# Attention and MLP on one Trainium2 core: unit 1's transposes in other PSUM banks, and an MLP step that splits its weights before its activation

## The chip, the core and the metric

The kernel runs on one core of a Trainium2 chip. Its engines are TensorE (PE, with its weight loads PEld), VectorE (DVE), ScalarE (ACT), GpSimd (POOL) and SyncE (SP); SP, ACT and POOL also issue transfers, named SPq, ACTq and POOLq. The metric is device microseconds of one execution. The profile is of one execution, and its span is the time from its first to its last instruction.

## What is computed

```
# decayed linear attention over blocks of 64, 2 x 8 heads, 768 tokens, 64 wide
intra = (qb @ kb.T * Dmask) @ vb ;  inter = (qb * lam_pow) @ kv_state
kv_state = lam**block * kv_state + (kb * rev_pow).T @ vb
x = attn_out as (1536 tokens, 512)
# MLP, 512 -> 2048 -> 512
h = max(x @ w_in, 0) ;  x = (h * h) @ w_out
# 8 experts, one per token by argmax(x @ w_gate), 512 -> 1024 -> 512
out[mask] = gate * sigmoid(x @ w_output_gate)[e] * (max(x[mask] @ w1[e], 0) @ w2[e])
```

All inputs arrive in fp32, apart from the MLP's two weights, which arrive as 64-bit floats and are converted on the chip.

## The kernel before

The program is written out in the order in which each engine takes its instructions (`manual_schedule`): an engine runs its own list strictly in that order and waits where an operand or a buffer isn't ready. Where a tile of a pool is given out again, its first writer waits for the last reader of the old one.

**Attention** runs over 12 units u (6 chunks of 128 tokens by 2 batches). Each has these steps: T(u) (`emit_T`) transposes q and k on PE into the PSUM tile psT, of which there is one, and ACT copies it to SBUF (four copies of 64x256 for q at L269, one of 128x512 for k at L272) and then issues the load of v (`load_v`, L190). S(u) (`emit_S`, L293) multiplies k by q into two PSUM tiles, of which there is one set, and DVE multiplies them by the decay mask into sm (L295). O(u) (`emit_O`) adds state by q (L312, from unit 2 on) and sm by v (L317); ACT writes the result's rounded part to xTh (L320), DVE the rest to xTl (L321). St(u) (`emit_St`, L343) updates the state. The loop over u runs T(u+2), S(u+1), O(u), St(u). Ahead of the loop stand T(0), T(1) and S(0), with warm-up products of the identity between them (`warm_pe`, L208) whose result is not used. q and k are loaded by SP (`load_qk`), four units ahead.

**The MLP** runs in three chunks of 512 tokens, each with 16 steps f over the hidden width, s = 16 chunk + f. Products are made with operands split in a rounded high and a low part: w_in's block into wih (a cast on ACT, L359) and wil (a subtraction, L360), by `split_in`; w_out's into woh and wol, by `split_out`. mm1(s) has 12 products of 128x512 (L372), mm2(s) 12 (L492). Between them `act1(s)` makes relu (r) and square (g) and splits g into gh (ACT) and gl (DVE). r and g have one buffer each, gh, gl, woh and wol two. mm2(s-2) stands behind mm1(s) on PE. In chunk 0 the weights are still arriving: SP loads pieces into four staging tiles st, ACT scales a piece (L134), DVE shifts and combines it (L135, L138, L142, the last two through `flush`), and only the end of L142 frees the staging tile for another load. wol is made by DVE in chunk 0 and by POOL after it.

After the MLP come the last chunk's routing (an early gather on POOL, L729 and L730, whose rows PE transposes at L741) and the experts.

Of the kernel before, what the change touches and what calls it, by code (L numbers as in the profile page):

```python
# [9 lines left out]
F32 = mybir.dt.float32  # L10
# [14 lines left out]
def attn_moe_kernel(ctx, tc, q, k, v, lam, w_in, w_out, w_gate, w_ogate, w1, w2, out):  # L25
    nc = tc.nc
    B, H, S, D = q.shape
# [159 lines left out]
    def load_v(u):  # L187
        b, c = units[u]
        tv = ldv.tile([P, H, D], F32, tag="v", name="v")
        nc.scalar.dma_start(out=tv, in_=v[b, :, c * P:(c + 1) * P, :].rearrange("h s d -> s h d"))  # L190
        qkv[u].append(tv)
# [14 lines left out]
    def warm_pe(n):  # L206
        for i in range(n):
            nc.tensor.matmul(out=pw_[:, i % HP, :], lhsT=ident, rhs=ident, start=True, stop=True)  # L208
# [43 lines left out]
    def emit_T(u):  # L252
        qt, kt = qkv[u][0:2]
        b, c = units[u]
        psT = pT.tile([P, 2, 2, HP, D], F32, tag="psT", name="psT")
        for hp in range(HP):
            for a in range(2):
                sl = slice(a * D, (a + 1) * D)
                nc.tensor.transpose(psT[:, a, 0, hp, :], qt[sl, hp, :], ident[sl, sl])
        for hp in range(HP):  # L260
            for a in range(2):
                sl = slice(a * D, (a + 1) * D)
                nc.tensor.transpose(psT[:, a, 1, hp, :], kt[sl, 2 * hp:2 * hp + 2, :].rearrange("p h d -> p (h d)"),
                                    ident[sl, sl])
        qT, kT = qT2[u % 2], kT2[u % 2]
        kv = kT.rearrange("p h (g t) -> p g h t", g=2)
        for a in range(2):
            for r in range(2):
                nc.scalar.copy(out=qT[a * D:(a + 1) * D, :, r::2], in_=psT[r * D:(r + 1) * D, a, 0])  # L269
                if u == a == r == 0:  # L270
                    load_v(u)
        nc.scalar.copy(out=kv, in_=psT[:, :, 1])  # L272
        if u > 0:
            load_v(u)
        kTs[u] = kT
        if c > 0:
            qd = wa.tile([P, HP, P], F32, tag="qd", name="qd")
            nc.gpsimd.tensor_tensor(out=qd, in0=qT, in1=lrow, op=ALU.mult)
            qds[u] = qd
        if c < NCH - 1:  # L280
            kd = wa.tile([P, H, D], F32, tag="kd", name="kd")
            nc.gpsimd.tensor_tensor(out=kd, in0=kt, in1=mask[:, :, P - 1:P].to_broadcast([P, H, D]), op=ALU.mult)
            kds[u] = kd
# [109 lines left out]
    def split_in(s, eng=nc.vector):  # L393
        f = s % NF
        wis[s] = split(wiF[:, :, f * P:(f + 1) * P], "wi", [P, KC, P], eng)
# [30 lines left out]
    powers(2, 32)  # L426
    emit_T(0)
    powers(32, P + 1)
    for t in state:
        nc.vector.memset(t, 0.0)  # L430
    warm_pe(4)
    load_qk(3)
    emit_T(1)
    emit_S(0)
    decays(0)
    decays(1)
    for u in range(NU):

        emit_tmp(u)
        wload(WL[u])  # L440
        if u + 4 < NU:
            load_qk(u + 4)
        if u + 2 < NU:
            emit_T(u + 2)
        if u == NU - 3:
            nc.sync.dma_start(out=tab.rearrange("(p n) w -> p (n w)", p=P), in_=tabi)
            sqk.close()
            sp[0] = sab.enter_context(tc.tile_pool(name="sp", bufs=2, side="right", reuse_waits="tile"))
        if u == NU - 2:
            split_in(0)  # L450
        if u < NU - 1:
            emit_S(u + 1)
        flush()
        if u == NU - 2:
            split_in(1)
        if u == NU - 1:
            mm1(0)
        emit_O(u)
        emit_St(u)
        if u == NU - 1:  # L460
            split_in(2)
        rest_ += wconv(WA[u], pO if u < NU - 3 else None)
# [352 lines left out]
    for s in range(NS + LAG):  # L815
        if s < NS:
            if s >= 2:
                mm1(s)
            early = 1 <= s < NF
            act1(s, lambda: (split_out(s - 1) if s else None, split_in(s + 2) if early else None, flush()))  # L820
        elif s == NS:
            split_out(s - 1)
        if NF <= s < NS - 2:
            split_in(s + 2)
        if wc[0] < NPC:
            wload(2)
            rest_ += wconv(2)
            if wc[0] == NPC:
                for i in range(4):
                    load_w1(i)  # L830
                    load_w2(i)
        if s >= LAG:
            mm2(s - LAG)
            ch, f = divmod(s - LAG, NF)
            if f == NF - 1:
                evac(ch)
            if ch > 0:
                for job in side.get(f, ()):
                    job(ch - 1)
            if ch == NCK - 1 and f == 10:  # L840
                slot_idx(slice(0, NSL), slice(0, 1))
        if s - 2 * NF in range(1, 9):
            i, j = divmod(s - 2 * NF - 1, 2)
            (split1, split2)[j](i)
        if s == NS - 1:
            early_gather()
            route_base(NCK - 1)
# [278 lines left out]
```

## Time and profile before

| | us |
|---|---|
| median of 3 runs | 556.07 (554.93 to 558.4) |
| the profiled execution | 556.97 |
| its span | 555.3 |
| PE busy | 539.7 (97%) |
| DVE busy | 336.2 (61%) |
| ACT busy | 303.6 (55%) |
| POOL busy | 148.3 (27%) |

Busy time is summed over the whole span, so it doesn't say which wait ends last in one stage; that is read from the chain of waits (followed back from the last instruction) and from the timeline of the stage. In the timeline a row's bracket is the time for which its engine stood idle before it, and what ended that.

### The profile page before, as it was taken

To read this page: it belongs to the slowest core of one execution; us is meant where nothing else is said; L and a number is where in the kernel's file an instruction comes from. 1 tells how busy PE (TensorE), PEld (TensorE's weight loads), DVE (VectorE), ACT (ScalarE), POOL (GpSimd) and SP (SyncE) were. 2 spreads that over 40 slices of the span, in tenths; PEclk is the share of its full clock that TensorE was granted. 3 is DMA by queue.
4 is the path that set the end of the run, shared out by engine and by line. 5 is a ranking of instruction groups with operands and counts; after the bars stand their busy time and mean duration, and the time that the engine had idled before them with its cause. 6 is when DMAs were issued, how large, how long until landed. Compare 5 with 4: busy or idle time off the path is not lost.

```text
span 555.3 us, 9744 instructions
## 1 busy us (share of the span) xinstructions
PE 539.7 (97%) x3599; PEld 460.7 (83%) x3599; DVE 336.2 (61%) x714; ACT 303.6 (55%) x577; POOL 148.3 (27%) x166
## 2 busy tenths in 40 slices
PE   7999999999999999999999989999999999999994
PEld 7899777778888878888888878889888889888983
DVE  3568998989645643344583327948264948975610
ACT  4668667776543444454554424447274857884610
POOL 8697000000021142312133250440313142240101
PEclk9999999999999999999999999999999999999998
DMA  8998545556500000000000003999538568930000
GB/s 201 218 244 224 152 154 200 180 192 231 221 1 2 24 34 19 1 0 1 19 20 19 21 17 129 377 199 394 183 127 284 206 201 262 293 123 20 10 21 25
DMA packets 75044, 72.88 MB, mean 131 GB/s; under 512 B 30181, under 2 KB 61029, under 8 KB 74976
## 3 DMA queue, kind: packets, MB, share of 16 engines
q1 hardware_dynamic: 58288, 59.91, 33.7%
q0 software_dynamic: 4064, 8.91, 5.0%
q10 hardware_dynamic: 12624, 3.15, 2.5%
q8 instruction: 43, 0.70, 0.5%
q14 instruction: 25, 0.20, 0.1%
HBM read 65.84 MB, written 9.29 MB: 135 GB/s over the span
## 4 chain that ended last, share of the span: by engine, by line
PE 73%; issue 12%; DVE 4%; DMA 4%; POOL 2%; ACT 2%; SPq 1%; POOLq 0%; ACTq 0%; DVEq 0%
PE acc L492 22%; PE ps L372 22%; PE ph L927 10%; PE ea L949 9%; DMA out_dram<-y,sidx 2%; PE ps L293 2%; PE po L312 1%; PE po L317 1%; DMA v<-in_v_dram 1%; DMA k<-in_k_dram 1%; POOL out_dram L959 1%; PE px L705 1%; SPq L182 1%; PE pt L906 1%; PE pt L343 1%
## 5 line engine op out<-in xcount | busy, mean ns | idle before, releaser
L360 POOL TENSOR_TENSOR wol<-woF,woh 128x512 fp32r<-128x512 f32 x32 | 41.1, 1285 | 222.8 <-ACT woh L359 222.8
L492 PE MATMUL acc<-gh,wol 128*128 128x512 f32 x192 | 76.4, 398 | 1.7 <-POOL wol L360 1.7
L927 PE MATMUL ph<-xh,xTh 128*128 128x192 f32 (+2 forms) x256 | 76.9, 301 | 0.9 <-DVE xl L912 0.4
L372 PE MATMUL ps<-xTh,wih 128*128 128x512 f32 x192 | 76.5, 398 | 0.0
L492 PE MATMUL acc<-gh,woh 128*128 128x512 f32 x192 | 75.0, 391 | 0.8 <-ACT woh L359 0.8
L372 PE MATMUL ps<-xTh,wil 128*128 128x512 f32 x192 | 74.9, 390 | 0.1
L492 PE MATMUL acc<-gl,woh 128*128 128x512 f32 x192 | 74.8, 390 | 0.0
L372 PE MATMUL ps<-xTl,wih 128*128 128x512 f32 x192 | 74.8, 389 | 0.0
L927 PE MATMUL ph<-xh,xTl 128*128 128x192 f32 (+2 forms) x256 | 74.7, 292 | 0.0
L927 PE MATMUL ph<-xl,xTh 128*128 128x192 f32 (+2 forms) x256 | 74.3, 292 | 0.0
L942 DVE SCALAR_TENSOR_TENSOR hl<-ph,hh 128x384 fp32r<-128x384 f32 (+1 forms) x64 | 34.5, 539 | 61.8 <-ACT hh L941 61.7
L390 DVE TENSOR_TENSOR gl<-g,gh 128x512 fp32r<-128x512 f32 x48 | 33.2, 691 | 58.8 <-ACT gh L389 58.8
L389 ACT CAST gh<-g 128x512 fp32r<-128x512 f32 x48 | 29.8, 620 | 52.7 <-PE acc L492 45.2
L927 PEld LDWEIGHTS ph<-xh,xTh 128*128 128x128 f32 x256 | 48.6, 190 | 7.0 <-DVE hl L942 4.9
L379 ACT ACTIVATE r<-ps 128x512 f32<-128x512 f32 x48 | 28.6, 595 | 44.7 <-PE ps L372 44.4
L941 ACT ACTIVATE hh<-ph 128x384 fp32r<-128x384 f32 (+1 forms) x64 | 30.9, 483 | 37.2 <-PE ph L927 34.0
L927 PEld LDWEIGHTS ph<-xl,xTh 128*128 128x128 f32 x256 | 48.6, 190 | 0.8
L927 PEld LDWEIGHTS ph<-xh,xTl 128*128 128x128 f32 x256 | 48.8, 191 | 0.2 <-DVE xTl L806 0.2
L886 POOL DMA_INDIRECT xg<-x1d,gidx x21 | 23.6, 1123 | 87.1 <-PE pt L906 62.3
L492 PEld LDWEIGHTS acc<-gh,wol 128*128 128x128 f32 x192 | 36.0, 188 | 12.9 <-DVE wol L360 3.7
L959 POOL DMA_INDIRECT out_dram<-y,sidx x23 | 23.6, 1028 | 76.9 <-ACT y L958 74.4
L806 DVE TENSOR_TENSOR xTl<-w1r,xTh 128x512 fp32r<-128x512 f32 x64 | 43.8, 689 | 0.1
(191 smaller groups left out, 1153.2 us busy)
## 6 DMA issues: line engine op xcount, KB each, us to landing
w1r<-in_moe_w_dram SPq DMA_DIRECT2D x32, 512.0 KB, 6.3
w2r<-in_moe_w_dram SPq DMA_DIRECT2D x32, 512.0 KB, 6.6
st<-in_moe_w_in_dram SPq DMA_DIRECT2D x16, 512.0 KB, 4.3
st<-in_moe_w_out_dram SPq DMA_DIRECT2D x16, 512.0 KB, 3.6
q<-in_q_dram SPq DMA_DIRECT2D x24, 128.0 KB, 4.5
k<-in_k_dram SPq DMA_DIRECT2D x12, 256.0 KB, 4.6
v<-in_v_dram ACTq DMA_DIRECT2D x12, 256.0 KB, 4.3
x1d<-xr SPq DMA_DIRECT2D x12, 256.0 KB, 2.0
```

The source lines that it names most:

```text
L360: eng.tensor_tensor(out=lo, in0=src, in1=hi.bitcast(F32), op=ALU.subtract)
L372: nc.tensor.matmul(out=ps, lhsT=w_[:, kk, :], rhs=x_[:, kk, tk], start=n == 0, stop=n == 3 * KC - 1)
L379: nc.scalar.activation(out=r, in_=ps, func=AF.Relu)
L389: nc.scalar.copy(out=gh, in_=g)
L390: nc.vector.tensor_tensor(out=gl, in0=g, in1=gh.bitcast(F32), op=ALU.subtract)
L492: nc.tensor.matmul(out=acc[ch][cb], lhsT=w_[:, cs], rhs=x_, start=f == 0 and i == 0, stop=f == NF - 1 and i == 2)
L806: eng.tensor_tensor(out=lo, in0=src, in1=hi.bitcast(F32), op=ALU.subtract)
L927: nc.tensor.matmul(out=ps[:, 0:N], lhsT=w_[:, kk, :], rhs=x_[:, kk, 0:N], start=n == 0, stop=n == 3 * KC - 1)
L941: nc.scalar.activation(out=hh[:, f, ts_], in_=ps[:, ts_], func=AF.Relu)
L942: nc.vector.scalar_tensor_tensor(out=hl[:, f, ts_], in0=ps[:, ts_], scalar=0.0, in1=hh[:, f, ts_].bitcast(F32), op0=ALU.max, op1=ALU.subtract)
L949: nc.tensor.matmul(out=ea[j], lhsT=h_[:, f, js], rhs=w_, start=f == 0 and i == 0, stop=f == NF2 - 1 and i == 2)
L959: nc.gpsimd.indirect_dma_start(out=outs[j][:, :], out_offset=bass.IndirectOffsetOnAxis(ap=sidx[:, j, e:e + 1], axis=0), in_=ys[j], in_offs ...
```

## The change

```
     def emit_T(u):
-        psT = pT.tile([P, 2, 2, HP, D], F32, tag="psT", name="psT")
+        if u == 1:
+            psa = [pm.tile([P, 2, HP, D], F32, tag="ps", name="psT1") for _ in range(2)]
+        else:
+            psT = pT.tile([P, 2, 2, HP, D], F32, tag="psT", name="psT")
+            psa = [psT[:, a] for a in range(2)]
...
+        if u == 0:
+            warm_pe(2)
...
+        copy = nc.vector.tensor_copy if u == 1 else nc.scalar.copy
         for a in range(2):
             for r in range(2):
-                nc.scalar.copy(out=qT[a * D:(a + 1) * D, :, r::2], in_=psT[r * D:(r + 1) * D, a, 0])
-                if u == a == r == 0:
-                    load_v(u)
-        nc.scalar.copy(out=kv, in_=psT[:, :, 1])
-        if u > 0:
-            load_v(u)
+                copy(out=qT[a * D:(a + 1) * D, :, r::2], in_=psa[a][r * D:(r + 1) * D, 0])
+        if u == 1:
+            for a in range(2):
+                copy(out=kv[:, a], in_=psa[a][:, 1])
+        else:
+            copy(out=kv, in_=psT[:, :, 1])
+        load_v(u)
...
-    for t in state:
-        nc.vector.memset(t, 0.0)
-    warm_pe(4)
+    warm_pe(7)
     load_qk(3)
     emit_T(1)
     emit_S(0)
+    for t in state:
+        nc.vector.memset(t, 0.0)
...
-        if u == NU - 2:
-            split_in(0)
         if u < NU - 1:
             emit_S(u + 1)
         flush()
-        if u == NU - 2:
-            split_in(1)
+        if NU - 3 <= u < NU - 1:
+            split_in(u - (NU - 3))
...
             if s >= 2:
                 mm1(s)
-            early = 1 <= s < NF
-            act1(s, lambda: (split_out(s - 1) if s else None, split_in(s + 2) if early else None, flush()))
-        elif s == NS:
-            split_out(s - 1)
+            if 1 < s <= NF:
+                split_out(s - 1)
+            if 1 <= s < NF:
+                split_in(s + 2)
+            act1(s, flush if s < NF else lambda: split_out(s))
+            if s == 0:
+                split_out(0)
```

T(1) gets two tiles of the pool that O and mm1 use, its copies go to DVE, the state's zeroing goes behind the first sm, and there are five more warm-ups. The splits of w_in's first two blocks come one unit earlier. In chunk 0 both splits of a step stand ahead of relu and square; in chunks 1 and 2 a step splits its own w_out block and not that of the step before.

On DVE, at the program's start (ca_142 is the mask in the first row and qT elsewhere, ca_141 is kT, ca_143 and ca_144 are the states), before:

```order
L215 SCALAR_TENSOR_TENSOR ca_142<-ca_141,ident 128x128 x8
L430 MEMSET ca_143 128x512
L430 MEMSET ca_144 128x512
L295 TENSOR_TENSOR sm<-ps,ca_142 128x4x128 x4
L321 TENSOR_TENSOR xTl<-po,xTh 128x4x128
```

and now:

```order
L215 SCALAR_TENSOR_TENSOR ca_142<-ca_141,ident 128x128 x8
L276 COPY ca_142<-psT_233 64x256 x2
L276 COPY ca_142<-psT_234 64x256 x2
L279 COPY ca_141<-psT_233 128x4x64
L279 COPY ca_141<-psT_234 128x4x64
L303 TENSOR_TENSOR sm<-ps,ca_142 128x4x128 x2
L442 MEMSET ca_143 128x512
L442 MEMSET ca_144 128x512
```

Six copies stand ahead of sm(0), and the two memsets between sm(0) and sm(1). On ACT, at the same place, before:

```order
L196 DMA ca_141<-in_lam_dram 128x8
L269 COPY ca_141<-psT 64x256
L190 DMA v<-in_v_dram 128x8x64
L269 COPY ca_141<-psT 64x256 x3
L272 COPY ca_141<-psT 128x2x4x64
L269 COPY ca_142<-psT 64x256 x4
L272 COPY ca_141<-psT 128x2x4x64
L190 DMA v<-in_v_dram 128x8x64
```

and now:

```order
L196 DMA ca_141<-in_lam_dram 128x8
L276 COPY ca_141<-psT 64x256 x4
L281 COPY ca_141<-psT 128x2x4x64
L190 DMA v<-in_v_dram 128x8x64 x2
L276 COPY ca_141<-psT 64x256 x4
```

The loads of v(0) and v(1) stand next to each other, ahead of unit 2's copies, with no copy of unit 1 before them. On ACT in chunk 0 of the MLP, steps 1 and 2, before:

```order
L379 ACTIVATE r<-ps 128x512
L382 ACTIVATE g<-r 128x512
L359 CAST woh<-woF 128x512
L359 CAST wih<-wiF 128x512
L389 CAST gh<-g 128x512
L134 ACTIVATE woF<-st 128x512
L134 ACTIVATE wiF<-st 128x4x128
```

and now:

```order
L367 CAST woh<-woF 128x512
L367 CAST wih<-wiF 128x512
L387 ACTIVATE r<-ps 128x512
L390 ACTIVATE g<-r 128x512
L397 CAST gh<-g 128x512
L134 ACTIVATE woF<-st 128x512
L134 ACTIVATE wiF<-st 128x4x128
```

The two splits moved from behind g to ahead of r. On POOL at the end of the MLP (xg is what the early gather brings), before:

```order
L623 DMA tab<-tg,sl 12288x2
L360 TENSOR_TENSOR wol<-woF,woh 128x512
L729 MEMSET xg_3602 128x512
L730 DMA xg_3602<-x1d,sidx 128x512
L729 MEMSET xg_3607 128x512
L730 DMA xg_3607<-x1d,sidx 128x512
L360 TENSOR_TENSOR wol<-woF,woh 128x512
```

and now:

```order
L629 DMA tab<-tg,sl 12288x2
L368 TENSOR_TENSOR wol<-woF,woh 128x512
L735 MEMSET xg_3613 128x512
L736 DMA xg_3613<-x1d,sidx 128x512
L735 MEMSET xg_3618 128x512
L736 DMA xg_3618<-x1d,sidx 128x512
L895 DMA xg<-x1d,gidx 128x512 x3
```

The last wol, that of step 47, stands ahead of the early gather and no longer behind it.

## Rows read from the trace of the kernel before

**Rows 1.** Page, the chain that ended last: shares of the span by engine.

```profile
PE 73%; issue 12%; DVE 4%; DMA 4%; POOL 2%; ACT 2%; SPq 1%; POOLq 0%; ACTq 0%; DVEq 0%
```

**Rows 2.** Chain in order of time, 0 to 90 us: start, us, what.

```profile
8.33 5.80 DMA k<-in_k_dram
...
14.14 6.28 DMA v<-in_v_dram
...
20.47 1.09 PE po L317 x16
...
23.61 1.02 PE po L312 x16
...
27.57 1.02 PE po L312 x16
28.59 0.87 PE po L317 x16
...
68.39 3.29 PE acc L492 x12
...
74.40 2.90 PE acc L492 x12
```

**Rows 3.** The same chain, 68 to 300 us.

```profile
144.19 2.72 PE ps L372 x12
```

**Rows 4.** Timeline, PE, 0 to 32 us: start, us, engine, line, op, operands, [idle before].

```profile
6.07 0.69 PE L263 MATMUL psT<-ident,k 64*128 64x64 f32 x8 [0.47 <-DMA k<-in_k_dram]
...
6.69 2.07 PE L208 MATMUL pw__157<-ident 128*128 128x128 f32 x8
...
9.37 0.69 PE L259 MATMUL psT<-ident,q 64*128 64x64 f32 x8 [0.61 <-ACT ca L272]
...
10.28 2.02 PE L293 MATMUL ps<-ca 64*128 64x128 f32 x16
...
18.57 1.11 PE L293 MATMUL ps<-ca 64*128 64x128 f32 x16
```

**Rows 5.** The same timeline, DVE: sm(0).

```profile
12.34 1.29 DVE L295 TENSOR_TENSOR sm<-ps,ca 128x512 f32<-128x512 f32 x2 [4.92 <-PE ps L293]
```

**Rows 6.** DVE by line and form, 14 to 56 us: xcount | busy, mean ns | idle.

```profile
L349 DVE COPY ca<-pt 64x256 f32<-64x256 f32 x4 | 1.7, 416 | 0.1
```

**Rows 7.** DMA issues at 4.84 (q), 6.27 (k) us: KB each, us to landing.

```profile
q<-in_q_dram SPq DMA_DIRECT2D x2, 128.0 KB, 3.5
...
k<-in_k_dram SPq DMA_DIRECT2D x1, 256.0 KB, 5.6
```

**Rows 8.** Stretches: length; PE, PEld, DVE, ACT, POOL busy; PEclk, DMA share, GB/s.

```profile
10.00:12.00 2.00, 2.00 (x26) 2.00 (x22) 0.00 (x0) 1.40 (x4) 1.96 (x3) 1.00 1.24 289
```

**Rows 9.** Timeline, 48 to 76 us: the MLP's first steps.

```profile
56.72 0.50 PE L372 MATMUL ps<-xTh,wih 128*128 128x512 f32 x1
...
57.51 0.19 PEld L372 LDWEIGHTS ps<-xTh,wil 128*128 128x128 f32 x1 [0.49 <-DVE wil L360]
...
66.14 0.69 DVE L390 TENSOR_TENSOR gl<-g,gh 128x512 fp32r<-128x512 f32 x1
...
68.39 0.50 PE L492 MATMUL acc<-gh,woh 128*128 128x512 f32 x1 [0.77 <-ACT woh L359]
```

**Rows 10.** Timeline, 66 to 82 us: wol of two steps on DVE.

```profile
73.95 0.69 DVE L360 TENSOR_TENSOR wol<-woF,woh 128x512 fp32r<-128x512 f32 x1 [0.59 <-ACT woh L359]
...
79.53 0.69 DVE L360 TENSOR_TENSOR wol<-woF,woh 128x512 fp32r<-128x512 f32 x1 [0.60 <-ACT woh L359]
```

**Rows 11.** Who waited for whom, PE: us in total, times, longest.

```profile
PE acc L492 <- POOL wol L360: 1.7, 1, 1.7
```

**Rows 12.** Timeline, ACT and POOL in chunks 1 and 2.

```profile
163.33 0.60 ACT L379 ACTIVATE r<-ps 128x512 f32<-128x512 f32 x1 [1.64 <-PE ps L372]
...
326.73 0.62 ACT L389 CAST gh<-g 128x512 fp32r<-128x512 f32 x1 [1.55 <-PE acc L492]
...
330.19 1.28 POOL L360 TENSOR_TENSOR wol<-woF,woh 128x512 fp32r<-128x512 f32 x1
```

More of the change, by code (lines that the diff above doesn't have):

```diff
@@ L258, in emit_T @@
                 sl = slice(a * D, (a + 1) * D)
-                nc.tensor.transpose(psT[:, a, 0, hp, :], qt[sl, hp, :], ident[sl, sl])
+                nc.tensor.transpose(psa[a][:, 0, hp, :], qt[sl, hp, :], ident[sl, sl])
+        if u == 0:
+            warm_pe(2)
         for hp in range(HP):
@@ L262, in emit_T @@
                 sl = slice(a * D, (a + 1) * D)
-                nc.tensor.transpose(psT[:, a, 1, hp, :], kt[sl, 2 * hp:2 * hp + 2, :].rearrange("p h d -> p (h d)"),
+                nc.tensor.transpose(psa[a][:, 1, hp, :], kt[sl, 2 * hp:2 * hp + 2, :].rearrange("p h d -> p (h d)"),
                                     ident[sl, sl])
```

## The prediction, made before the changed kernel ran

> **What bounds the kernel now.** I read the chain of waits first. PE's own work is 73% of the span [rows 1], and PE is busy for 97% of it, so the only things worth removing are places where PE stands still or runs slowly. The chain in order of time shows three of them where the change works, and I read the timeline of each.
>
> The first is the head. The chain there is no computation but the load of v(1), issued on ACT's queue at 14.14 and landed 6.28 us later; only from O(1) at 20.47 is it PE without a gap [rows 2]. PE also works at half its speed in the head: the same 16 products of S take 2.02 us at 10.28 and 1.11 us at 18.57 [rows 4]. The column of the granted clock reads 1.00 there [rows 8], so the low level (1.2 GHz against 2.4) is read from the durations and not from that column. PE had not gone without a pause until then: it idled 0.47 us for k(0) and 0.61 us at 9.37, where T(1) waits for ACT to empty the only psT [rows 4].
>
> The second is chunk 0 of the MLP. From the start of mm1(0) at 56.72 [rows 9] to the end of mm2(13) at 144.19 [rows 3] are 87.47 us. In it lie 16 mm1 and 14 mm2 at 2.72 us when nothing is late [rows 3], and O(11) at 1.02 + 0.87 [rows 2]: 30 x 2.72 + 1.89 = 83.49 us. So 3.98 us are lost: mm1(0) waits for wil [rows 9], mm2(0) starts 0.77 us late for woh [rows 9] and takes 3.29 us for want of wol, and each of the 13 mm2 behind it takes 2.81 to 2.90 us like the one at 74.40 [rows 2].
>
> The third is 1.7 us, once, at the MLP's end: PE waits for POOL's last wol [rows 11], which POOL begins at 330.19 [rows 12] behind the early gather.
>
> **The change, part by part.** *Head.* T(1) no longer waits for psT, but it stands behind more warm-ups and its copies are on DVE. Eight rows of a warm-up group of four take 2.07 us [rows 4], nearly 0.2 of it the last one's tail, so about 0.47 us each at the low clock. T(0)'s q part ends at 5.6 as before; two warm-ups end at 6.5 and T(0)'s k part (0.65) at 7.15, k(0) having landed at 6.07 [rows 4]. Seven warm-ups end at 10.45. I take it that the clock rises about then, PE having worked from 1.44 without a pause; T(1) took 0.91 us at the low clock (9.37 to 10.28 [rows 4]), and I take 0.75: its end is 11.2. DVE's copies are then on the path. It has four of 64x256, at 416 ns by its own copy out of PSUM [rows 6], and two of 128x256, for which I take the same since each partition has as many elements: 2.5 us, end 13.7. sm(0), which DVE began at 12.34, begins only now, takes 1.29 [rows 5] and ends at 15.0. S(0) (1.11) and T(2) lie beside the copies. S(1) writes the tiles that sm(0) reads, so its second half waits: end 16.0. O(0) starts there, and O(1) one steady unit later, 3.96 us between two L312 [rows 2], less the L312 of 1.02 that unit 0 doesn't have: 18.95. Against 20.47 that is **1.5 us gained**. The memsets (1 us) lie between sm(0) and sm(1), while PE makes S(1), O(0) and T(3), and cost nothing; without that cover they would cost 1 us.
>
> v has to be there. Before, v(1) goes out when k(3), of the same semaphore, has landed (8.33 + 5.80, then 14.14 [rows 2]). In the changed program v(0)'s load shares its semaphore with q(2)'s and v(1)'s with k(2)'s. q(2) was issued at 4.84 and landed 3.5 us later, k(2) at 6.27 and 5.6 [rows 7]: v(0) goes out at about 8.4 (7.04 before) and v(1) at 11.9 instead of 14.14. With 6.3 us to land, v(1) is there at 18.2, v(0) before 15; both in time, v(1) by 0.7 us. While ACT's queue stands at v(1) until 11.9, unit 2's copies stand behind it, but T(2) ends only at about 12.7.
>
> Here a rule speaks against the change. The DMA engines are full between 10 and 12 us (share 1.24, 289 GB/s [rows 8]). The Trainium skill, "DMA: Bandwidth & Descriptors", section "Issuing engines are not separate DMA queues", says that transfers begun by several engines run on the same 16 DMA engines and interleave, so that where they are issued saves only issue time. By it an earlier v(1) gains no bandwidth, and if its bytes still came at 20.4 the head would give nothing and the sum would be 4.7 us. I go by the row: the bytes queued ahead of an issue at 11.9 are fewer than those ahead of one at 14.14.
>
> Bounds of the head: if the clock rises early in the seven warm-ups (0.235 us each from then on), T(1) ends at 9.4, S(1) at 14.2, and O(1) is held by v(1) at 17.9: +2.6. If it doesn't rise before O(0), S(1) ends at 17.0 and O(0) takes 0.9 longer: O(1) at 20.8, -0.35.
>
> *Chunk 0.* A DVE step from wol to wol takes 79.53 - 73.95 = 5.58 us, of which 0.60 is waiting for woh [rows 10]; its work is 4.98 us, less than PE's 2 x 2.72 = 5.44. The wait comes from woh standing behind g, which waits for the previous gl. With woh ahead of r it is gone, and PE sets the pace: the 0.1 to 0.2 us in each mm2 goes, except at the start, where DVE has a backlog. I walked that: DVE's order is the same up to gl(0) at 66.14 [rows 9], then wol(0) ends at 67.4, while mm2(0), now starting at 66.8 because wil(0) is long made, wants it at 67.2; wol(1) is 0.25 late likewise; from then on DVE gains 0.46 us a step. Of the 3.98 us I leave 0.5 for this and 0.5 for mm2 rows that were a little slow without a wait: **3.0 us gained** (bounds: 3.9 if nothing is left; 1.6 if wol stays 0.1 late in 14 steps and the start gives only what it must). wil(0), moved one unit ahead on DVE, delays xTl(9) by 0.6 us; mm1(0)'s buffer needs xTl(9), which would end at 56.25, before 56.72. The staging loop has slack: a piece loaded 4 us after its tile is freed is wanted two steps, 10.9 us, after the last.
>
> *End of the MLP.* woh(47) now waits for mm2(45), as gh(47) already did at 326.73 [rows 12], so wol(47) is ready at 326.7 + 0.6 + 1.28 = 328.6 and PE wants it near 329.9: **1.7 us gained** (1.2 if the gather, 2.1 us later on POOL, comes just late). Every step of chunks 1 and 2 has woh on ACT between mm2(s-2) and gh, 0.5 us; ACT idles 1.64 us before the next r [rows 12], so it costs nothing while that lasts.
>
> Sum: 1.5 + 3.0 + 1.7 = 6.2 us. The span goes from 555.3 to 549.1, the profiled execution (1.67 us more) from 556.97 to 550.8; the median was 0.9 below that, so 556.07 - 6.2 = **549.9**.
>
> **The rivals.** *v(1) still sets O(1).* For it: the full DMA engines; against it: v(1) leaves 2.2 us earlier. Sum 4.7, time 551.4. *The clock stays low.* For it: nothing in the head before raised it by 10.4; against: PE then paused twice. The head loses 0.35: sum 4.35, time 551.7. *Chunk 0's wait only moves*, from woh to the staged weights or DVE's queue: ACT then stands at a load and DVE behind it. For it: DVE's 4.98 us leaves only 0.46 a step. The start still gives 1.2: sum 4.4, time 551.7. *Slower:* in chunks 1 and 2 the wait of woh(s) for mm2(s-2) pushes gh, wih and wil late enough that mm1 waits in all 31 steps. It decides from 0.38 us a step ((5.6 + 6.2) / 31); at 0.4 the time is 549.9 + 12.4 = 562.3. Against it: wil(s+2) would be ready some 2.4 us after mm2(s-2), and mm1(s+2) starts 5.44 us after it, so 3 us would have to go wrong.
>
> **How the numbers follow.** Forecast 0.60, with its own range 548 to 551; v(1) sets O(1) 0.15; chunk 0's wait moves 0.14; the clock stays low 0.07; slower by ACT 0.04. One per cent is 5.6 us, about what a measurement of this kernel can tell from no change; that is a time of 550.5, and the forecast is only 0.6 below it. Most of the forecast's case (0.53) and a little of the others (0.02) fall below it: faster 0.55, within 1% 0.41, slower 0.04. The range takes in the bounds, from 556.07 - 8.2 = 547.9 to 556.07 - 2.4 = 553.7, cut to 547.5 to 553.5 for 8 in 10, a run's scatter at the low end included.
>
> **What would show it.** Head: T(1) follows the warm-ups with no wait, sm(0) starts near 13.7, O(1) near 19, and S at 1.1 us by S(1). If PE waits for v at O(1), the first rival holds. Chunk 0: no wait of DVE for woh, the mm2 of the chain at 2.72 to 2.78 from the third on. End: no wait of PE for POOL's wol, and none for the gathered rows instead. I am wrong if a gap reappears behind the place where one went: S(1) later than 16, ACT at a load in chunk 0, or PE at the gathered rows near 335.

## The result, and the profile after

| | before | after |
|---|---|---|
| median | 555.55 us (6 runs, 554.55 to 558.4) | 551.07 us (6 runs, 550.61 to 551.57) |
| profiled execution, its span | 556.97, 555.3 | 551.02, 549.3 |
| ratio after to before | | 0.9915, 95% interval 0.9893 to 0.9936 |

The changed kernel is faster by 0.85%, some 4.5 us (3.6 to 5.9 by the interval). That is clear of no change, but it lies within the 1% to which the prediction gave 0.41, where it gave a larger gain 0.55. The forecast was 549.9 us, 6.2 below the median known then; 551.07 lies in the stated range (547.5 to 553.5) and just outside the forecast case's own (548 to 551). Between the two profiled executions the gain is 6.0 us of span, but the one of before lay 1.4 us above its median of six runs.

The lines of the code have moved: transposes L263 and L269 (before L259 and L263), copies L276 to L281, S L301, sm L303, O L320 and L325, splits L367 and L368, mm1 L380, gl L398, mm2 L498, the copy of a chunk's result to x1T L508 (ACT) and L510 (DVE), routing product pl L529, the early gather L735 and L736, its transposes L747.

Who waited for whom on PE after the change (us in total, times, longest), where it concerns these places:

```profile
PE ps L301 <- DVE sm L303: 1.7, 1, 1.7
...
PE acc L498 <- DVE x1T L510: 0.5, 2, 0.3
```

The three waits of before are gone: for v ahead of O(1) [rows 2], for woh ahead of mm2(0) [rows 9] and for POOL's last wol [rows 11]. Two waits for x1T are new. They are small, and they are where the forecast was wrong.

**The head.** Timeline of PE after (start us, us, line, operation, operands, idle before):

```profile
6.52 0.47 PE L269 MATMUL psT<-ident,k 64*128 64x64 f32 x8
6.92 1.83 PE L208 MATMUL pw__157<-ident 128*128 128x128 f32 x14
8.68 0.46 PE L263 MATMUL psT<-ident,q 64*128 64x64 f32 x8
...
12.65 2.56 PE L301 MATMUL ps<-ca,ca 64*128 64x128 f32 x16 [1.68 <-DVE sm L303]
15.14 1.89 PE L325 MATMUL po<-sm,v 128*64 128x128 f32 x16
...
19.02 1.09 PE L325 MATMUL po<-sm,v 128*64 128x128 f32 x16
```

O(1) starts at 19.02 against 20.47 [rows 2], 1.45 us earlier, as forecast (18.95), but by another way, so that in this profile the agreement is luck. T(1) starts at 8.68, not at 10.45: the clock was up by the end of the first pair of warm-ups (k(0)'s transposes behind it take 0.47 us), so that the seven behind them took 1.83 us, little more than half of what I had allowed. Then most of S(1) and O(0) ran slowly (O(0) 1.89 us against 1.09 for O(1)) and gave it back.

Behind T(1) stand DVE's copies and sm(0), 1.79 + 0.76 + 1.28 us, and v(1) is issued at 10.45; timeline of ACT and DVE after:

```profile
8.53 0.38 ACTq L190 DMA_DIRECT2D v<-in_v_dram  x1
...
9.42 1.79 DVE L276 COPY ca<-psT 64x256 f32<-64x256 f32 x4 [3.09 <-PE psT L269]
...
10.45 0.44 ACTq L190 DMA_DIRECT2D v<-in_v_dram  x1
...
11.24 0.76 DVE L279 COPY ca<-psT 128x256 f32<-128x256 f32 x2
11.91 1.28 DVE L303 TENSOR_TENSOR sm<-ps,ca 128x512 f32<-128x512 f32 x2
```

**Chunk 0 and the last wol.** The chain of waits after, in order of time (start us, us, what):

```profile
65.82 2.75 PE acc L498 x12
...
71.30 2.85 PE acc L498 x12
...
76.87 2.72 PE acc L498 x12
...
320.44 8.16 PE acc L498 x36
328.60 1.21 PE pl L529 x32
```

mm2(0) takes 2.75 us instead of 3.29, the second 2.85, and from the third on they take 2.72, where the mm2 of before behind its first took 2.81 to 2.90 (the one at 74.40 in [rows 2] has 2.90). The last three mm2 stand in one piece of 8.16 us, 3 x 2.72, with no wait for wol in it.

**The ends of the chunks, which are new.** Timeline of POOL, DVE and PE around the end of chunk 0 after:

```profile
150.82 1.29 POOL L368 TENSOR_TENSOR wol<-woF,woh 128x512 fp32r<-128x512 f32 x1 [4.15 <-ACT woh L367]
...
151.30 1.37 DVE L398 TENSOR_TENSOR gl<-g,gh 128x512 fp32r<-128x512 f32 x1 [2.29 <-ACT gh L397]
...
152.59 0.68 DVE L368 TENSOR_TENSOR wil<-wiF,wih 128x512 fp32r<-128x512 f32 x1
...
153.19 1.27 DVE L510 COPY x1T<-acc 128x512 f32<-128x512 f32 x2
...
153.92 0.50 PE L498 MATMUL acc<-gh,woh 128*128 128x512 f32 x1 [0.21 <-DVE x1T L510]
```

gl takes 1.37 us, where it took 0.69 [rows 9]. It lies beside POOL's wol. x1T stands two places behind it on DVE, and PE wants the accumulators that x1T empties: between two products that elsewhere start 0.23 us apart lie 0.60 us here (153.32 to 153.92).

From mm1(0) to the last chunk's routing nothing scatters: in every kernel run here the same stretch with the same code took the same time to 0.03 us. So the gain can be split by three landmarks of the chain: pl(0), pl(1), pl(2), the start of the routing product behind each chunk's last mm2.

| us | start of mm1(0) | to pl(0) | to pl(1) | to pl(2) |
|---|---|---|---|---|
| before | 56.72 | 109.23 | 91.25 | 76.92 |
| after | 55.25 | 106.45 | 91.81 | 75.09 |
| difference | -1.47 | -2.78 | +0.56 | -1.83 |

Chunk 0 shows its own gain less its end's loss; the next section tells them apart. The other 0.5 us of the span's 6.0 lie behind pl(2), where the experts' code is the same in every kernel here. That part scatters: from pl(2) to the end it takes 221.2 us before, 220.7 after, and 220.5 to 222.5 over the fourteen profiles of this study.

### The profile page after: what moved, and what is told of

Its sections match the earlier page's. It is cut to its first block, busy times and chain, and to the rows that moved or that the text cites. A ratio compares the mean times of both kernels' runs of the same rounds, so it can differ in the third digit from the quotient of the medians.

```text
span 549.3 us, 9807 instructions
## 1 busy us (share of the span) xinstructions
PE 536.7 (98%) x3609; PEld 460.9 (84%) x3609; DVE 356.6 (65%) x720; ACT 302.8 (55%) x572; POOL 150.7 (27%) x166
## 4 chain that ended last, share of the span: by engine, by line
PE 84%; issue 9%; DVE 3%; POOL 1%; DMA 1%; ACT 1%; POOLq 0%; ACTq 0%
PE acc L498 24%; PE ps L380 23%; PE ph L936 13%; PE ea L958 11%; PE ps L301 2%; PE po L325 2%; PE po L320 2%; PE pw__157 L208 1%; PE px L711 1%; POOL out_dram L968 1%; PE pt L915 1%; PE pt L351 1%; PE psT L263 1%; DMA out_dram<-y,sidx 1%; PE pl L529 1%
## 5 line engine op out<-in xcount | busy, mean ns | idle before, releaser
L368 POOL TENSOR_TENSOR wol<-woF,woh 128x512 fp32r<-128x512 f32 x32 | 41.4, 1292 | 219.4 <-ACT woh L367 219.4
L398 DVE TENSOR_TENSOR gl<-g,gh 128x512 fp32r<-128x512 f32 x48 | 52.6, 1097 | 68.7 <-ACT gh L397 68.7
L380 PE MATMUL ps<-xTh,wih 128*128 128x512 f32 x192 | 76.5, 398 | 0.0
L498 PE MATMUL acc<-gh,woh 128*128 128x512 f32 x192 | 75.0, 390 | 0.5 <-DVE x1T L510 0.5
L498 PE MATMUL acc<-gh,wol 128*128 128x512 f32 x192 | 74.8, 390 | 0.0
L380 PE MATMUL ps<-xTl,wih 128*128 128x512 f32 x192 | 74.8, 390 | 0.0
L380 PE MATMUL ps<-xTh,wil 128*128 128x512 f32 x192 | 74.8, 389 | 0.0
L498 PE MATMUL acc<-gl,woh 128*128 128x512 f32 x192 | 74.7, 389 | 0.0
L367 ACT CAST woh<-woF 128x512 fp32r<-128x512 f32 x48 | 29.6, 617 | 56.5 <-PE acc L498 56.5
L498 PEld LDWEIGHTS acc<-gh,woh 128*128 128x128 f32 x192 | 36.0, 188 | 8.7 <-DVE x1T L510 1.3
```

The lines of the kernel that those rows point to most:

```text
L367: nc.scalar.copy(out=hi, in_=src)
L368: eng.tensor_tensor(out=lo, in0=src, in1=hi.bitcast(F32), op=ALU.subtract)
L380: nc.tensor.matmul(out=ps, lhsT=w_[:, kk, :], rhs=x_[:, kk, tk], start=n == 0, stop=n == 3 * KC - 1)
L398: nc.vector.tensor_tensor(out=gl, in0=g, in1=gh.bitcast(F32), op=ALU.subtract)
L498: nc.tensor.matmul(out=acc[ch][cb], lhsT=w_[:, cs], rhs=x_, start=f == 0 and i == 0, stop=f == NF - 1 and i == 2)
```

## The experiments

Twelve kernels ran, in three sets of four, each set beside before on one chip.

| kernel | median us | before, same chip | ratio, 95% interval |
|---|---|---|---|
| e1_head | 556.31 | 556.39 | 0.9987 [0.9964, 1.0009] |
| e2_chunk0 | 553.29 | 556.39 | 0.9938 [0.9913, 0.9963] |
| e3_late | 555.57 | 556.39 | 0.9966 [0.9944, 0.9987] |
| e4_lastonly | 550.32 | 556.39 | 0.9882 [0.9843, 0.9920] |
| e6_warm4 | 551.10 | 555.59 | 0.9922 [0.9898, 0.9946] |
| e7_fill | 551.53 | 555.59 | 0.9915 [0.9897, 0.9933] |
| e8_dvewol | 550.47 | 555.59 | 0.9896 [0.9879, 0.9914] |
| e9_best | 549.45 | 555.59 | 0.9887 [0.9867, 0.9906] |
| e10_kvact | 549.18 | 556.46 | 0.9862 [0.9840, 0.9884] |
| e11_nohead | 551.17 | 556.46 | 0.9892 [0.9869, 0.9915] |
| e12_last2 | 550.23 | 556.46 | 0.9878 [0.9858, 0.9899] |
| e13_kvwarm4 | 547.94 | 556.46 | 0.9849 [0.9826, 0.9872] |

### The three parts, one at a time

**e1_head** is the changed kernel with the MLP's order, and the splits in attention, of before.

> The kernel before with the head's part alone (unit 1's tiles and copies, warm-ups, memsets, the order of v's loads). Theory: the head's gain stands by itself, 1.45 us as in the changed kernel: O(1) starts at 19.0, TensorE stands 1.7 us ahead of S(1) waiting for sm(0), and S(1) takes 2.0 us again; the time falls 1.5 us below the kernel before. Rival: the attention's later units are set by the loads or by VectorE, and the gain is given back before the MLP: mm1(0) at 56.7 and no change of the time.

**e2_chunk0** is before with both splits of chunk 0 ahead of relu and square, and w_in's first two splits one unit earlier:

```diff
-        if u == NU - 2:
-            split_in(0)
...
+        if NU - 3 <= u < NU - 1:
+            split_in(u - (NU - 3))
...
+            if 1 < s <= NF:
+                split_out(s - 1)
+            if 1 <= s < NF:
+                split_in(s + 2)
+            act1(s, flush if s < NF else lambda: split_out(s - 1) if s > NF else None)
+            if s == 0:
+                split_out(0)
```

> The kernel before with the part in the MLP's chunk 0 alone (both splits ahead of relu, the first two splits of w_in one unit earlier); chunks 1 and 2 as before. Theory: 3.3 us are gained between O(11) and the end of mm2(13), every mm2 from the third on takes 2.72 us in the chain, VectorE waits for no woh; the time falls by 3.3 us. Rival: part of what the changed kernel shows in chunk 0 comes from its earlier start (the staged weights arrive relatively earlier): then the gain is 2 us or less and some mm2 stay at 2.8.

**e3_late** is before with `split_out(s)` of its own step, ahead of gh, in chunks 1 and 2 alone:

```diff
-            act1(s, lambda: (split_out(s - 1) if s else None, split_in(s + 2) if early else None, flush()))
-        elif s == NS:
-            split_out(s - 1)
+            if s == NF:
+                split_out(s - 1)
+            act1(s, (lambda: (split_out(s - 1) if s else None, split_in(s + 2) if early else None, flush())) if s < NF
+                 else lambda: split_out(s))
```

> The kernel before with the part in chunks 1 and 2 alone (a step splits its own block of w_out). Theory: gl on VectorE takes 1.3 us in place of 0.69 because GpSimd's wol now runs beside it; at each of the two chunk ends the copies of the accumulators come late and TensorE loses about 0.5 us, 1.1 us together; TensorE doesn't wait for the last wol, 1.8 us gained; sum 0.7 us faster. Rival: the loss at the chunk ends is not of this part, gl stays at 0.69 us and the sum is 1.8 us.

Measured by the landmarks:

| us | start of mm1(0) | to pl(0) | to pl(1) | to pl(2) |
|---|---|---|---|---|
| before | 56.72 | 109.23 | 91.25 | 76.92 |
| e1_head | 55.62 | 109.24 | 91.25 | 76.93 |
| e2_chunk0 | 55.43 | 105.94 | 91.26 | 76.92 |
| e3_late | 56.38 | 109.77 | 91.81 | 75.06 |

In these stretches the parts don't touch each other. Chunk 0 is worth 109.23 - 105.94 = 3.29 us, and the ratio of e2_chunk0 says 3.4 (2.1 to 4.8). e3_late loses 0.54 + 0.56 at the two chunk ends and gains 1.86 at the end, 0.76 in all; its medians differ by 0.82, its ratio says 0.7 to 3.1. e1_head's mm1(0) is 1.1 us earlier, but its median is before's: the head is the part that one profile and twelve runs don't settle (its ratio says between 2.0 us faster and 0.5 slower). In its profile the 1.1 us are lost again behind pl(2), in a tail of 222.5 us against 221.2. And e2_chunk0, with before's head, started mm1(0) as early as the head change does.

### Why gl takes twice as long

**e4_lastonly** is the changed kernel with chunks 1 and 2 in the order of before, and only the last `split_out` ahead of the gather:

```diff
-            act1(s, flush if s < NF else lambda: split_out(s))
-            if s == 0:
-                split_out(0)
+            act1(s, flush if s < NF else lambda: split_out(s - 1) if s > NF else None)
+            if s in (0, NS - 1):
+                split_out(s)
```

> The changed kernel with chunks 1 and 2 in the order of before (the block of the step before is split behind g), and only the last block's split of step 47 put ahead of the early gather. Theory: gl takes 0.69 us again, the two chunk ends lose nothing, the last wol still costs no wait: 1.1 us faster than the changed kernel, 5.5 us faster than the kernel before. Rival: the late chunk ends are from something else (ScalarE's longer list), TensorE still loses 0.5 us at each, and the time is that of the changed kernel.

**e8_dvewol** keeps woh ahead of gh on ACT, as the changed kernel has it, but DVE makes wol at the end of the step (behind `evac`), so that only POOL's part is taken away (`wo_hi` makes woh, `wo_lo` makes wol):

```diff
...
-            act1(s, flush if s < NF else lambda: split_out(s))
+            act1(s, flush if s < NF else lambda: wo_hi(s))
...
                 evac(ch)
+            if NF <= s < NS:
+                wo_lo(s)
```

> The changed kernel with woh still ahead of gh on ACT in chunks 1 and 2, but wol made by VectorE at the end of the step instead of by POOL. Theory (gl takes 1.1 to 1.4 us because POOL's wol runs beside it, and this lateness is what PE waits for at the two chunk ends): gl takes 0.69 us, x1T of the chunk ends is copied 0.7 us earlier after its accumulators, PE does not wait there, each chunk end takes 0.5 us less (22.27 to 21.75 and 91.81 to 91.25 us between the landmarks), the time is 1.1 us below the changed kernel's, near 550.0. Rival (woh's 0.6 us on ACT ahead of gh is what costs): the two stretches stay at 22.27 and 91.81 whatever gl takes, the time stays at 551.1.

The page's row of gl (xcount | busy us, mean ns | idle before), after:

```profile
L398 DVE TENSOR_TENSOR gl<-g,gh 128x512 fp32r<-128x512 f32 x48 | 52.6, 1097 | 68.7 <-ACT gh L397 68.7
```

e4_lastonly:

```profile
L398 DVE TENSOR_TENSOR gl<-g,gh 128x512 fp32r<-128x512 f32 x48 | 33.1, 690 | 62.7 <-ACT gh L397 62.7
```

e8_dvewol:

```profile
L398 DVE TENSOR_TENSOR gl<-g,gh 128x512 fp32r<-128x512 f32 x48 | 33.1, 690 | 66.8 <-ACT gh L397 66.8
```

48 gl, of which 16 lie in chunk 0. In the timeline of after, 29 of the other 32 take 1.36 to 1.38 us; each of these starts 0.47 to 0.48 us into a wol of POOL and ends 0.55 us behind that wol's end. The other three have no wol beside them and take 0.69 us, as the 16 of chunk 0 do. Timeline of POOL and DVE after, near one of the three:

```profile
186.25 1.29 POOL L368 TENSOR_TENSOR wol<-woF,woh 128x512 fp32r<-128x512 f32 x1 [4.14 <-ACT woh L367]
...
189.03 0.69 DVE L398 TENSOR_TENSOR gl<-g,gh 128x512 fp32r<-128x512 f32 x1 [0.74 <-ACT gh L397]
```

In e8_dvewol woh stands on ACT ahead of gh as after, DVE's idle time for gh is nearly the same (66.8 us against 68.7), and every gl takes 0.69 us. So POOL's wol beside it is what doubles it, and the doubled gl, not the 0.5 us that woh takes on ACT, is what PE waits for: the two chunk ends of e8_dvewol and of e4_lastonly lose nothing (105.92 and 105.93 to pl(0), 91.26 each to pl(1)). Their times point the same way without settling it, since the intervals overlap: by the ratios e8_dvewol lies 0.0019 x 556 = 1.1 us below the changed kernel, as forecast, and e4_lastonly 1.8 us, by the medians 0.6 and 0.75. Doubled gl inside a chunk cost next to nothing: the last stretch, to pl(2), which holds eleven of them, is 75.09 us after and 74.93 in both of these.

The order of before had kept the two apart. ACT made woh(s-1) behind r(s), and so POOL's wol lay in the gap between DVE's g and gl; timeline of before in chunk 1:

```profile
158.52 0.69 DVE L384 TENSOR_TENSOR g<-r,ps 128x512 f32<-128x512 f32 x1 [0.26 <-ACT r L379]
159.07 1.28 POOL L360 TENSOR_TENSOR wol<-woF,woh 128x512 fp32r<-128x512 f32 x1 [4.16 <-ACT woh L359]
...
161.20 0.69 DVE L390 TENSOR_TENSOR gl<-g,gh 128x512 fp32r<-128x512 f32 x1 [2.00 <-ACT gh L389]
```

wol ends at 160.35, gl starts at 161.20; only the last 0.14 us of g lie beside wol, and g isn't longer for it. After the change gl starts 0.48 us into a wol of 1.29 and takes 1.37.

The Trainium skill, "SBUF — State Buffer", section "Who interferes with whom", states it as a rule: a VectorE instruction with two SBUF inputs contends with a GpSimd instruction that reads SBUF, over ports under an exclusive lock, and the one that starts second is blocked until the first is done. By that rule gl would end at 150.82 + 1.29 + 0.69 = 152.80; it ended at 151.30 + 1.37 = 152.67, so the trace agrees to 0.13 us. The prediction weighed another page's rule and missed this one.

### What the head is worth

**e11_nohead** is e4_lastonly with the head of before, and **e12_last2** is e4_lastonly again, on the same chip.

> e4_lastonly with the head of before: both splits of chunk 0 early and the last wol ahead of the gather, nothing else. Theory (the change of the head gains less than the 1.45 us between the two profiled executions, since the clock and v's landing vary from execution to execution): 0.5 to 1.0 us above e4_lastonly's time of the same chip. Rival 1 (it gains what the two traces showed): 1.5 us above. Rival 2 (it gains nothing): the same time.

> e4_lastonly once more, as the kernel that e10_kvact, e11_nohead and e13_kvwarm4 are measured against on the same chip: 549.5 to 550.5 us, ratio to before 0.988 to 0.990. If it came out 1 us or more away from its first 550.3, differences of that size between sessions would say nothing.

551.17 against 550.23: by these the change of the head is worth about 0.9 us, by the two ratios 0.8, and by the ratio of e1_head 0.7. None of the three is clear of noise (the six runs of e11_nohead reach from 549.56 to 552.11, and the two intervals overlap), so 0.7 to 0.9 is what they say best, and neither 0 nor the 1.45 us between two profiles is ruled out. e12_last2 repeated e4_lastonly's median to 0.1 us.

e4_lastonly and e12_last2 are one and the same kernel. Their profiles show why a profile of the head isn't enough. Timeline of PE in e4_lastonly:

```profile
6.71 0.69 PE L269 MATMUL psT<-ident,k 64*128 64x64 f32 x8
7.33 3.25 PE L208 MATMUL pw__157<-ident 128*128 128x128 f32 x14
...
10.52 0.46 PE L263 MATMUL psT<-ident,q 64*128 64x64 f32 x8
...
14.48 1.75 PE L301 MATMUL ps<-ca,ca 64*128 64x128 f32 x16 [1.82 <-DVE sm L303]
16.16 1.09 PE L325 MATMUL po<-sm,v 128*64 128x128 f32 x16
...
19.24 1.09 PE L325 MATMUL po<-sm,v 128*64 128x128 f32 x16
```

and in e12_last2 (timeline of PE, then the stretch from 13.42 to 16.80 us with its busy times, the granted clock as the last column but two, DMA share and GB/s):

```profile
6.61 0.47 PE L269 MATMUL psT<-ident,k 64*128 64x64 f32 x8
7.00 1.83 PE L208 MATMUL pw__157<-ident 128*128 128x128 f32 x14
...
12.73 2.60 PE L301 MATMUL ps<-ca,ca 64*128 64x128 f32 x16 [1.69 <-DVE sm L303]
15.26 1.85 PE L325 MATMUL po<-sm,v 128*64 128x128 f32 x16
...
19.09 1.09 PE L325 MATMUL po<-sm,v 128*64 128x128 f32 x16
```

```profile
13.42:16.80 3.38, 3.38 (x28) 3.16 (x30) 2.17 (x4) 0.00 (x0) 0.83 (x1) 0.50 0.95 232
```

Eight transposes of k(0) take 0.69 us at the low level (1.2 GHz) or 0.47 at the high one (2.4 GHz). The trace keeps its own list of changes of the granted clock, and that agrees. In the first execution the clock rose at 10.35, at the end of the seven warm-ups, which is the case of the prediction; in the second at 6.60, and from 13.43, behind PE's idle time of 1.69 us and early in S(1), it was at the low level (0.50) again until 16.84. The two ways end within 0.15 us of each other. In the fourteen profiles of this study k(0)'s transposes took 0.69 us in seven and 0.46 or 0.47 in seven, with the old head and the new. In the first seven the rise stands at 17.46 to 17.75 with the head of before (before, e3_late, e11_nohead) and at 10.35 to 10.90 with the changed one (e1_head, e4_lastonly, e7_fill, e9_best); in the other seven at 4.31 to 6.60. The Trainium skill, "TensorE: Matmul & The Clock Gate", section "What's actually happening", says that the point at which the clock rises differs from run to run of the same kernel; these rows agree.

With before's head an early clock brings e2_chunk0 to where the changed head is. Timeline of PE in e2_chunk0:

```profile
6.04 0.46 PE L263 MATMUL psT<-ident,k 64*128 64x64 f32 x8 [0.43 <-DMA k<-in_k_dram]
...
9.41 0.46 PE L259 MATMUL psT<-ident,q 64*128 64x64 f32 x8 [1.82 <-ACT ca L272]
...
19.20 1.09 PE L317 MATMUL po<-sm,v 128*64 128x128 f32 x16 [1.26 <-DMA v<-in_v_dram]
```

O(1) starts at 19.20, having waited 1.26 us for v(1). So the old head was held by v(1)'s load where the clock was early, and at 20.1 to 20.5 by PE at the low level and v(1) together where it was late (20.47 before, 20.11 in e3_late, 20.13 in e11_nohead, with waits for v(1) of 0.79, none and 0.18 us).

So like can be laid beside like. Where the clock rises late, O(1) starts at 20.11 to 20.47 with the old head and at 19.24 to 19.44 with the new: 0.7 to 1.2 us gained, by a clock that is up 7 us earlier. Where it rises early, O(1) starts at 19.20 with the old head (one profile) and at 19.02 and 19.09 with the new (a third, e8_dvewol's, lost 3 us to a wait for v(0), of which more below): 0.1 to 0.2 us. The 1.45 us between the two first profiles are a late execution of before against an early one of after.

### Warm-ups: more, fewer, elsewhere

**e6_warm4** is the changed kernel with before's four warm-ups instead of two and seven:

```diff
-        if u == 0:
-            warm_pe(2)
...
-    warm_pe(7)
+    warm_pe(4)
```

> The changed kernel with 4 warm-ups between T(0) and T(1), in one group as before, instead of 2 + 7. Theory (what the head gains comes from T(1)'s own PSUM banks and the copies on VectorE, not from more warm-ups): T(1) starts at about 8.6 us, at the low level it takes 0.9 us, the copies end at 12.0, sm(0) at 13.3, S(1) at the low level ends at about 14.5, O(0) at 16.4, O(1) at 18.5 to 19.3 us, so the time is that of the changed kernel, 551.1, within 0.5 us. Rival (the extra warm-ups are what raises the clock): S(0), S(1) and O(0) take 2.0 us each and T(3), S(2) are slow too, O(1) starts at 20 us or later, the time is 1 to 1.5 us above the changed kernel's.

The median is the theory's: 551.10 against 551.07, ratios 0.9922 and 0.9915. But the six runs lie at 548.8 to 550.2 and at 552.1 to 553.2, further apart than the changed kernel's (550.6 to 551.6), so the median stands for neither group. The one profile is of the fastest run. In it the clock rose at 4.31, before the place where the warm-ups differ, PE paused 0.51 us for k(0), and O(1) started at 16.51:

```profile
6.01 0.47 PE L267 MATMUL psT<-ident,k 64*128 64x64 f32 x8 [0.51 <-DMA k<-in_k_dram]
...
16.51 1.09 PE L323 MATMUL po<-sm,v 128*64 128x128 f32 x16
```

So where the clock is up that early the added warm-ups aren't needed for it. Whether they are what raises it at 10.35 to 10.90 in the other kind, as the rival has it, stays open: no profile shows this kernel with a late clock, and its three slower runs lie 1 to 2 us above the changed kernel, about where the rival puts them.

**e7_fill** fills PE's idle 1.7 us ahead of S(1) with six warm-ups, and **e9_best** does so on top of e4_lastonly:

```diff
         if u + 2 < NU:
             emit_T(u + 2)
+        if u == 0:
+            warm_pe(6)
```

> The changed kernel with 6 more warm-ups (1.4 us at the high level) in the 1.7 to 1.8 us in which PE stands idle before S(1). Theory (that idle time is why S(1) and O(0) ran at the low level in the changed kernel's profile, 1.96 and 1.89 us): S(1) and O(0) take 1.1 us each; O(1) starts at 17.5 to 18.7 us instead of 19.0 to 19.4, the time is 0.5 to 1.5 us below the changed kernel's 551.1. Rival 1: the clock's level has nothing to do with that idle time, S(1) and O(0) stay slow, the time stays. Rival 2: O(1) only waits for v(1) instead, which landed at 17.05: then a wait of PE for the load of v stands ahead of O(1) and it starts near 19.

> The changed kernel with chunks 1 and 2 in the order of before (only the last wol ahead of the early gather, as in e4_lastonly) and with the 6 warm-ups before S(1). Theory: the two gains add, chunk ends lose nothing (21.75 and 91.25 us), O(1) starts at 17.5 to 18.7 us: 0.5 to 1 us below e4_lastonly's 550.3, so 549.3 to 549.8, some 6.5 us (1.2%) below before. Rival: the warm-ups bring nothing, the time is e4_lastonly's 550.3.

Neither gains by it: e7_fill's ratio is the changed kernel's 0.9915, e9_best's 0.9887 is e4_lastonly's within its interval. Timeline of PE in e7_fill:

```profile
12.79 1.60 PE L208 MATMUL pw__157<-ident 128*128 128x128 f32 x12
14.68 1.75 PE L301 MATMUL ps<-ca,ca 64*128 64x128 f32 x16 [0.28 <-DVE sm L303]
...
19.44 1.09 PE L325 MATMUL po<-sm,v 128*64 128x128 f32 x16
```

S(1) still takes 1.75 us, because its second half waits for sm(0)'s second half, as the prediction had it; that is DVE's time and no clock's. Both profiles fell in the kind where the clock rises late, and there it stayed up over 1.8 us of idle time even without the fill (e4_lastonly above). So what makes it fall again in the other kind isn't shown, and whether the fill would prevent that wasn't seen. It fell behind idle times of 1.68 (after) and 1.69 us (e12_last2) and within one of 2.54 us (e8_dvewol), and not behind 1.82 us in e4_lastonly and in e2_chunk0; the length of the pause alone doesn't decide it.

### Taking the head's own path shorter

With the warm-ups done, the chain of the head runs through DVE: four q copies (1.79 us after), two k copies (0.76), sm(0) (1.28), then S(1)'s second half. **e10_kvact** is e4_lastonly with the k copies on ACT:

```diff
             for a in range(2):
-                copy(out=kv[:, a], in_=psa[a][:, 1])
+                nc.scalar.copy(out=kv[:, a], in_=psa[a][:, 1])
```

> e4_lastonly with T(1)'s two k copies on ACT instead of VectorE (the four q copies stay). Theory (with the clock up, the head runs through VectorE: 1.8 us of q copies, 0.76 us of k copies, sm(0) 1.28 us, then the second half of S(1)): sm(0) starts about 0.75 us earlier after T(1), S(1) ends as much earlier, O(1) starts 0.5 to 0.75 us earlier than in e4_lastonly; time 0.5 us below e4_lastonly's of the same chip. Rival: v(1)'s load or the clock sets O(1) by then and the time is e4_lastonly's.

**e13_kvwarm4** is that with four warm-ups, as in e6_warm4.

> e10_kvact with 4 warm-ups between T(0) and T(1), in one group, instead of 2 + 7. Theory: where the clock is up by 6 us, T(1) comes 2 us earlier and O(1) starts at 16 us (as in e6_warm4's profile, 16.51); where it isn't, S(0) and S(1) run at the low level; on the mean the two cancel and the time is e10_kvact's within 0.5 us, with a wider scatter of runs. Rival: the extra warm-ups decide when the clock rises, and without them the time is 1 us or more above.

e10_kvact is 1.05 us below e12_last2, by more than the theory said. In its profile O(1) runs into the wait that the prediction had as its first rival: v(1) is issued at 11.79, 1.3 us later than after (10.45). The k copies ahead of that issue on ACT explain the way to 11.0, where the second of them starts. Behind it ACT stands 0.90 us until a load of q lands: by the trace's records of the issues v(1)'s load shares its semaphore in this program with the second load of q(3), which lands at 11.77, and no longer with k(2)'s, which lands at 10.37. ACT and PE in e10_kvact:

```profile
11.79 0.37 ACTq L190 DMA_DIRECT2D v<-in_v_dram  x1
12.27 1.62 ACT L276 COPY ca<-psT 64x256 f32<-64x256 f32 x4 [0.90 <-DMA q<-in_q_dram]
```

```profile
11.78 1.66 PE L301 MATMUL ps<-ca,ca 64*128 64x128 f32 x16 [0.90 <-DVE sm L303]
...
18.13 1.09 PE L325 MATMUL po<-sm,v 128*64 128x128 f32 x16 [1.36 <-DMA v<-in_v_dram]
```

e13_kvwarm4 was to equal e10_kvact and came out 1.24 us below it: 547.94 us, 1.5% below before, the best of all, and 2.3 us below the kernel of the same order with the added warm-ups and DVE's k copies (e12_last2). T(1) starts at 7.76 in its profile, O(1) at 16.49, mm1(0) at 52.73 (ACT's issue of v(1) first, then PE):

```profile
10.55 0.38 ACTq L190 DMA_DIRECT2D v<-in_v_dram  x1
```

```profile
7.76 0.46 PE L263 MATMUL psT<-ident,q 64*128 64x64 f32 x8
...
16.49 1.09 PE L323 MATMUL po<-sm,v 128*64 128x128 f32 x16
```

The fewer warm-ups are not the whole of the 1.24 us. Here v(1)'s load waits for k(2)'s semaphore again, goes out at 10.55 and is there in time, where e10_kvact's O(1) had waited 1.36 us for it; without that wait e10_kvact's would have started near 16.8. What each of the two is worth wasn't measured apart. Nor do these profiles show a gain from the k copies on ACT: e6_warm4, with four warm-ups and the k copies on DVE, started O(1) at 16.51. The clock rose early in this profile too (4.78); what its late kind costs wasn't seen in a trace.

## Why the prediction was right or wrong, point by point

**The sum.** 1.5 + 3.0 + 1.7 = 6.2 us was forecast. Measured apart, the parts are 0.9 (head, e11_nohead against e12_last2, not clear of noise), 3.3 (chunk 0), 1.8 (last wol) and -1.1 (chunk ends), 4.9 together, against 3.6 to 5.9 by the ratio of the whole. The forecast missed by two terms, the chunk ends' 1.1 us, which the landmarks show, and the head's 0.6, which is less certain; chunk 0 and the last wol gave 0.4 us more than I had said.

**Head, +1.5, measured about 0.9.** The mechanism held: T(1) without a wait for psT, DVE's copies 2.55 us (2.5 forecast), S(1)'s second half bound to sm(0). In executions where the clock rises late its numbers came true one by one: T(1) from 10.52 (10.45), S(1) to 16.2 (16.0), O(1) at 19.24 (18.95) in e4_lastonly. In those executions the gain is 0.7 to 1.2 us, in early ones 0.1 to 0.2. The step that failed is the comparison with 20.47: that was one execution of a head which reached O(1) at 19.2 in another. I took one profile for the mean, and a stretch whose clock level isn't the same in every execution has no such single value. The bound +2.6 (clock rises early in the seven) was worked out with O(1) at 17.9; the clock did rise early in the changed kernel's profile, even before the seven, but fell again at 13.41, which I hadn't allowed for.

**v.** v(0) was issued at 8.53 (8.4 forecast) and v(1) at 10.45, where I had said 11.9, since k(2) landed earlier than I had it. The first rival didn't occur in the changed kernel's profile: no wait for v stands in its list. It is near, though: e8_dvewol's profiled execution, with the same head, waited 2.54 us for v(0) and started mm1(0) at 58.42, three us later than the others, and e10_kvact waited 1.36 us for v(1):

```profile
16.80 1.97 PE L325 MATMUL po<-sm,v 128*64 128x128 f32 x16 [2.54 <-DMA v<-in_v_dram]
```

(timeline of PE in e8_dvewol). The rule on issuing queues that was weighed there isn't tested by this: no run changed the queue and left the time of issue.

**Clock stays low.** It didn't: with the changed head and seven warm-ups the clock had risen by 10.90 in all eight profiles. In four of them it rose at 10.35 to 10.90, where the forecast had put it, in the other four at 4.79 to 6.60, which it had only as a bound. The two profiles with four warm-ups (e6_warm4, e13_kvwarm4) had it up at 4.31 and 4.78, before the place where the warm-ups differ, so they don't tell whether the seven are needed.

**Chunk 0, +3.0, measured 3.29.** Right in mechanism: mm2(0) at 2.75, the second at 2.85, then 2.72. Of the 0.5 us that I had kept for mm2 that are slow without a wait, most wasn't there: the excess over 2.72 of the first two is 0.16 us. No wait of PE moved to the staging.

**Last wol, +1.7, measured 1.83.** Right, and the gathered rows weren't late: the last gather was issued on POOL at 327.64 and PE reached their transposes at 331.65 without a wait.

**"Costs nothing while that lasts", measured -1.1.** This is the step that failed. For woh ahead of gh in chunks 1 and 2 I looked at ACT's idle 1.64 us [rows 12] and at PE's next mm1, and found room. I didn't ask what the earlier woh releases: POOL's wol, which then starts 0.48 us ahead of gl and runs into it, where before it started 2.13 us ahead and was done. My rival for the slower side had the right place and the wrong mechanism (ACT's queue rather than POOL beside DVE) and looked for its price in every step, where there was slack, and not at the two chunk ends, where x1T stands behind gl.

## What to carry to other kernels

When an instruction is moved earlier on one engine, follow what it releases on the others, and lay that against what runs there now: an off-path POOL operation moved beside a DVE operation cost 1.1 us at the two chunk ends, where the moved cast itself cost nothing. Slack found in a loop's steady steps must be looked for again at the loop's ends. Price a stretch whose clock level differs from execution to execution from several executions, or from a pair of kernels that differ in nothing else, never from one profile of each. Before a load's delay is put down to the instructions ahead of it, look at which other load's semaphore it shares: that can change with the order of the program.

## What the runs showed of the hardware that I had not expected

A VectorE subtraction of 128x512 with both inputs in SBUF took 1.37 us instead of 0.69 when a GpSimd subtraction of the same form had started 0.48 us earlier, in 29 of 29 cases after; that is 0.68 us more, of the 0.82 for which the GpSimd one still ran, and the GpSimd one kept its duration (1.29 us, 1.28 before). So here the one that started second paid for the overlap; the other order is not shown here.

The same kernel had TensorE's clock up at 6.60 us in one execution and only at 10.35 in another, and in the early kind it could be down again at 13.4. Behind the head, from mm1(0) at about 55 us to the last chunk's routing at about 328, two executions of the same code agree to 0.03 us; nearly all of the scatter between executions lies ahead of and behind that stretch.
